# GpSimd forms the low parts of the blocks of w3 and the products r·k·u of three more chunks

## The chip, the cores and the metric

The kernel runs on one core of one Trainium2 chip. The metric is the device time of one execution in microseconds (us). The kernel before took 889.52 us (median of 3 runs, 889.01 to 890.25).

A core has five engines that each work through their own list of instructions in order and wait for one another by semaphores: TensorE (PE in the rows, its weight loads PEld), VectorE (DVE), ScalarE (ACT), GpSimd (POOL) and SyncE (SP), which here only issues DMAs.

## The reference

Three layers follow each other. A linear attention runs over 768 steps with a state per head:

```
for t in range(S):
    cur = einsum('bhd,bhe->bhde', u * k[t], v[t])
    y[t] = einsum('bhd,bhde->bhe', r[t], state + cur)
    state = w[t][..., None] * state + einsum('bhd,bhe->bhde', k[t], v[t])
```

Its output x (3072 rows of 384) goes through `h = ((x @ w1) * (x @ w2)) @ w3` and `h @ w_out`, and then through a mixture of eight experts with two chosen per row. All of it is float32.

## The kernel before

float32 matrices are multiplied in three passes. A matrix is split in a high part h (the value rounded to the narrower format `fp32r`) and a low part l = x - h, and `mm3` (lines 182 to 184) issues three matmuls: high by high, high by low, low by high. For each tile of a weight, ScalarE prepares the bits (`top`, line 153), VectorE joins them into a float (`cvz`, line 166), ScalarE rounds it (h, line 168), and VectorE subtracts (l, line 173). This is `cvt` with its queue `flush`: a call of `cvt` for the next tile first issues the join of the tile before and the subtraction of the tile before that.

The kernel folds w3 and w_out into one matrix first. In the loop over u (0 to 18) `cv_wo(u)` converts one of 8 blocks of w_out (`WBh`, `WBl`), `cv_w3(u)` one of 16 blocks of w3 (`w3h`, `w3l`, 128 x 512, three buffers each, with four buffers of `cvz`), and `mm_w3(u - 3)` multiplies: 12 matmuls of 400 columns, of which the four of line 184 read `w3l`. I count blocks of w3 from 0 to 15.

The attention works on 24 chunks of 128 steps, counted from 0 too, two per group of 256 rows. Steps of the first chunks are laid between the folding's by a table of times: `pre_scan` (`fg`), `pre_rec` (`rc`, `kt`), `pre_k`, `pre_r` (`rt`), then `pre_u` (lines 240 to 245), which forms r·k·u in two multiplications of 128 x 384 into the tile `rku` (one buffer), `pre_c` (line 250, `cc`, the sum over a head's columns), `pre_d` (line 256: ScalarE lays `cc` on the diagonals of `am`, eight instructions), `at_A` (line 263), `do_ov` (line 268, VectorE), `at_y` (line 332, the output, rounded into `xh` by ScalarE at line 338 and `xl` by VectorE at line 339) and `at_kv` (line 296, the state). After `pre_u(j)` follows the load of r and k for chunk j + 2 (`nrk`, two buffers). In the kernel before, VectorE forms the products for chunks 2, 3 and 4, GpSimd those of all others.

From 66 us on the groups' matmuls with w1, w2 and the folded matrix run (`mo_ab`, `mo_x`), in between the attention's; then the experts.

VectorE's instructions stand in the order in which the program issues them. Those of TensorE (until the third group), ScalarE, GpSimd and SyncE are put in order by a scheduler with costs of its own, so a changed engine for one instruction can reorder the others.

Of the kernel before, what the change touches and what calls it, by code (L numbers as in the profile page):

```python
# [16 lines left out]
OP = mybir.AluOpType  # L17
# [3 lines left out]
DM, FF, E = 384, 1024, 8  # L21
# [50 lines left out]
def tile_kernel(ctx: ExitStack, tc: tile.TileContext, dt, nat, w3t, wout, w1, w2, e1, e2, cf, ci, out):  # L72
    nc = tc.nc
    pe, act, dve, pool, sp = nc.tensor, nc.scalar, nc.vector, nc.gpsimd, nc.sync
# [6 lines left out]
    class Pinned:  # L81
        on = False
# [7 lines left out]
    def f(ap):  # L90
        return ap.bitcast(F32)
# [14 lines left out]
    def c(n):  # L106
        o, w = CF[n]
        return cft[:, o:o + w]
# [32 lines left out]

    CQ, LQ, TOP = [], [], [cvp.tile([P, 512], I32, name=f"top{i}", bufs=1) for i in range(2)]

    def cvt(rw, n, h, l, o=0, post=None):

        t = TOP[0][:, :n]
        TOP.append(TOP.pop(0))  # L150
        top = rw.bitcast(BF16)[:, 4 * o + 4:4 * o + 4 * n + 4].rearrange("p (n t) -> p n t", t=4)[:, :, 0]
        mid = rw[:, 2 * o + 1:2 * o + 2 * n + 1].rearrange("p (n t) -> p n t", t=2)[:, :, 0]
        act.activation(out=t.bitcast(F16).rearrange("p (n t) -> p n t", t=2)[:, :, 1], in_=top, func=AF.Copy)
        z = cvp.tile([P, 512], I32, name="cvz")[:, :n]
        if post == "z":
            dve.scalar_tensor_tensor(z, mid, 13, t, op0=OP.logical_shift_right, op1=OP.bitwise_or)
            return z.bitcast(F32)
        flush(1)
        CQ.append((mid, t, z, h, l, post))

    def flush(n=2):
        for _ in range(n):
            low, LQ[:] = LQ[:], []
            while CQ:
                mid, t, z, h, l, post = CQ.pop()
                dve.scalar_tensor_tensor(z, mid, 13, t, op0=OP.logical_shift_right, op1=OP.bitwise_or)  # L166
                x = z.bitcast(F32)
                (act.copy if xo_ else dve.tensor_copy)(out=h, in_=x)
                LQ.append((h, l, x))
                if post:  # L170
                    post(x)
            for h, l, x in low:
                dve.tensor_tensor(out=l, in0=x, in1=f(h), op=OP.subtract)  # L173

    def load64(rw, src):

# [10 lines left out]
    DT, RK, VV, FG, RC, KT, RT, AM, KN, XH, XL, KS = ({} for _ in range(12))  # L187
# [51 lines left out]

    def pre_u(j):  # L240
        t = att.tile([P, DM], F32, name="rku", bufs=1)
        on = dve if 2 <= j < 5 else pool
        on.tensor_tensor(out=t, in0=RK[j][:, :DM], in1=RK[j][:, DM:], op=OP.mult)  # L243
        on.tensor_tensor(out=t, in0=t, in1=c("u"), op=OP.mult)
        KS["u", j] = t

    def pre_c(j):
# [104 lines left out]
    def do_u(j):  # L352
        pre_u(j)
        if j + 2 < NCH:
            load_rk(j + 2)
# [29 lines left out]
    rawx, w3s, xo_, R1 = {}, {}, {}, {}  # L385
# [10 lines left out]
    def cv_wo(j):  # L396
        cvt(rawx["o", j], DM, woh[:, j, :DM], wol[:, j, :DM], post=lambda x: xo_.__setitem__(j, x))
# [18 lines left out]

    def cv_w3(u):
        w3s[u] = [fold.tile([P, 512], F32R, name=x, bufs=3) for x in ("w3h", "w3l")]
        cvt(rawx["3", u], 512, *w3s[u])

    def mm_w3(u):
        jb = u % 8
# [18 lines left out]
    def cv_w(m, fp, i):  # L441
        sl = slice(768 * fp + 384 * i, 768 * fp + 384 * i + 384)
        rw, o = piece(m, fp, i)
        cvt(rw, 384, (WAh, WBh)[m][:, sl], (WAl, WBl)[m][:, sl], o)

    def cv_early():
        flush(1)
        for i in range(2):
            rw, o = piece(1, 0, i)
            EZ.append(cvt(rw, 384, None, None, o, "z"))  # L450
# [51 lines left out]
    for i, fn in enumerate(STEPS):  # L502
        for j in range(NCH):
            late = 3 if j == NCH - 1 and i == 1 else 0
            at(WHEN[j][i] if j in WHEN else 6 * j - 14 + LATE[i] - late, fn, j)
    at(-3, flush)
    at(-3, flush, 1)
    for slot in (0.1, 2.55, 2.9, 3, 5, 5.3, 6.02, 6.04):
# [24 lines left out]
    for u in range(19):  # L533
        if u < 8:
            cv_wo(u)
            ld_raw()
        if u < 16:
            cv_w3(u)
            ld_raw()
        elif u == 16:  # L540
            flush()
        run_todo(u - 24, u - 23.5)
        if u > 2:
            mm_w3(u - 3)
        if 0 < u < 9:
            gate_cols(u - 1)
            gate_split(u - 1)
        if u == 1:
            warm_up(6)
        if u < 8:  # L550
            wo_T(u)
        if u == 0:
            warm_up(3)
        act.on = u >= 15
        run_todo(u - 23.5, u - 23)
# [591 lines left out]
    if RMAX > 1:  # L1147

        n = nc.values_load(rounds[0:1, E:E + 1], min_val=1, max_val=RMAX)
# [102 lines left out]
```

## Time and profile before

| | |
|---|---|
| median of 3 runs | 889.52 us |
| profiled execution | 888.03 us, its span 886.1 us |
| PE busy | 866.6 us (98%) |
| DVE busy | 496.2 us (56%) |
| ACT busy | 434.8 us (49%) |
| POOL busy | 244.2 us (28%) |

The span reaches from the first to the last instruction that the profiler saw. An engine's busy time counts its instructions alone, not its waits. Averages over the span say little about the first 112 us, to which the change belongs: there VectorE is busy most of the time and GpSimd hardly. The times of a row are from the span's start.

### The profile page before, as it was taken

How to read it: one execution, taken by the hardware profiler on the slowest of the kernel's cores; microseconds unless marked ns; L12 is line 12 of the kernel's file. 1: busy time of each engine (PE TensorE's matmuls, PEld its weight loads, DVE VectorE, ACT ScalarE, POOL GpSimd, SP SyncE). 2: the span in 40 equal slices, each digit the busy share in tenths (PEclk: the TensorE clock that was granted, in tenths of full speed). 3: DMA queues.
4: the chain of work that ended last, by engine and by line, in shares of the span. 5: the costliest groups of instructions: out<-in, count | busy, mean ns of one | idle time of the engine just before them, and what ended most of it. 6: DMA issues, size and time to landing. Idle time of an engine off the chain costs nothing.

```text
span 886.1 us, 18270 instructions
## 1 busy us (share of the span) xinstructions
PE 866.6 (98%) x7333; PEld 807.6 (91%) x7333; DVE 496.2 (56%) x1215; ACT 434.8 (49%) x876; POOL 244.2 (28%) x216
## 2 busy tenths in 40 slices
PE   8999999999999999999999999999999999999994
PEld 5889899999999999999989989899998989999894
DVE  6899866857756766666474453443434344353320
ACT  5787576566466546645454343334334343434320
POOL 2000020141131231231453434326061341604022
PEclk9999999999999999999999999999999999999998
DMA  9965398465475563525186786829287583835113
GB/s 344 405 221 178 99 135 267 119 201 162 129 205 170 157 170 109 147 70 157 43 205 126 177 244 190 196 83 226 57 228 138 145 202 91 221 76 110 18 22 38
DMA packets 123967, 139.22 MB, mean 157 GB/s; under 512 B 74976, under 2 KB 103648, under 8 KB 123872
## 3 DMA queue, kind: packets, MB, share of 16 engines
q1 hardware_dynamic: 100336, 109.58, 43.1%
q0 software_dynamic: 12160, 19.72, 11.9%
q10 hardware_dynamic: 11376, 8.65, 3.0%
q8 instruction: 59, 0.97, 0.5%
q14 instruction: 36, 0.29, 0.1%
HBM read 88.12 MB, written 36.04 MB: 140 GB/s over the span
## 4 chain that ended last, share of the span: by engine, by line
PE 87%; DVE 5%; DMA 3%; ACT 1%; issue 1%; POOL 0%; SPq 0%; POOLq 0%; ACTq 0%; DVEq 0%
PE pb L182 27%; PE pb L183 26%; PE pb L184 26%; PE pb L332 3%; PE pb L263 3%; DMA rawf<-wout 2%; PE pb L932 1%; DMA nrk<-nat 1%; PE pb L296 1%; DVE cvz L166 1%; DMA rawf<-w 1%; DVE am L268 0%; DVE WAl L173 0%; DVE fg L210 0%; DVE w3l L173 0%
## 5 line engine op out<-in xcount | busy, mean ns | idle before, releaser
L937 POOL DMA_INDIRECT out<-ye,ti x49 | 77.0, 1572 | 225.2 <-ACT ye L927 204.8
L910 DVE SCALAR_TENSOR_TENSOR HH<-pb,HH 128x256 fp32r<-128x256 f32 (+1 forms) x128 | 71.2, 557 | 112.3 <-ACT HH L909 112.3
L182 PE MATMUL pb<-XTh,WAh 128*128 128x512 f32 (+1 forms) x384 | 131.7, 343 | 0.0
L184 PE MATMUL pb<-XTh,WAl 128*128 128x512 f32 (+1 forms) x384 | 131.3, 342 | 0.0
L183 PE MATMUL pb<-XTl,WAh 128*128 128x512 f32 (+1 forms) x384 | 131.0, 341 | 0.0
L182 PE MATMUL pb<-WBh,HH 128*128 128x384 f32 x384 | 129.3, 337 | 0.0
L184 PE MATMUL pb<-WBh,HH 128*128 128x384 f32 x384 | 128.4, 334 | 0.0
L183 PE MATMUL pb<-WBl,HH 128*128 128x384 f32 x384 | 128.3, 334 | 0.0
L909 ACT ACTIVATE HH<-pb 128x256 fp32r<-128x256 f32 (+1 forms) x128 | 62.8, 492 | 115.4 <-PE pb L184 113.3
L742 POOL DMA_INDIRECT slots<-g_sc,g_si x48 | 51.6, 1074 | 127.1 <-DVE g_si L741 71.6
L927 ACT ACTIVATE ye<-pb,ti 128x384 f32<-128x384 f32 x42 | 24.4, 582 | 124.2 <-PE pb L184 124.2
L183 PE MATMUL pb<-xl,WAh 128*128 128x256 f32 x288 | 80.9, 281 | 0.8 <-DVE xl L339 0.8
L182 PE MATMUL pb<-xh,WAh 128*128 128x256 f32 x288 | 81.5, 284 | 0.0
L183 PE MATMUL pb<-xl,WBh 128*128 128x256 f32 x288 | 81.0, 281 | 0.0
L182 PE MATMUL pb<-xh,WBh 128*128 128x256 f32 x288 | 81.0, 281 | 0.0
L184 PE MATMUL pb<-xh,WBl 128*128 128x256 f32 x288 | 81.0, 281 | 0.0
L184 PE MATMUL pb<-xh,WAl 128*128 128x256 f32 x288 | 80.8, 281 | 0.0
L183 PEld LDWEIGHTS pb<-XTl,WAh 128*128 128x128 f32 x384 | 72.3, 188 | 7.6
L184 PEld LDWEIGHTS pb<-XTh,WAl 128*128 128x128 f32 x384 | 72.2, 188 | 7.5
L182 PEld LDWEIGHTS pb<-XTh,WAh 128*128 128x128 f32 x384 | 72.0, 188 | 7.5
L182 PEld LDWEIGHTS pb<-WBh,HH 128*128 128x128 f32 x384 | 72.1, 188 | 5.0 <-ACT WAh L810 4.4
L243 POOL TENSOR_TENSOR rku<-nrk 128x384 f32<-128x384 f32 x21 | 21.7, 1031 | 194.3 <-DVE cc L250 79.4
(203 smaller groups left out, 2065.1 us busy)
## 6 DMA issues: line engine op xcount, KB each, us to landing
dtc<-dt SPq DMA_DIRECT2D x24, 772.0 KB, 5.2
raw<-e SPq DMA_DIRECT2D x18, 768.0 KB, 5.9
raww<-e SPq DMA_DIRECT2D x14, 768.0 KB, 5.5
nrk<-nat SPq DMA_DIRECT2D x24, 384.0 KB, 5.5
expert_rows<-xg SPq DMA_DIRECT2D x45, 192.0 KB, 4.1
rawf<-w3t SPq DMA_DIRECT2D x16, 512.0 KB, 7.5
nv<-nat SPq DMA_DIRECT2D x24, 256.0 KB, 4.5
out<-zeros SPq DMA_DIRECT2D x9, 576.0 KB, 4.5
```

What stands on the lines that cost most here:

```text
L166: dve.scalar_tensor_tensor(z, mid, 13, t, op0=OP.logical_shift_right, op1=OP.bitwise_or)
L182: pin(pe.matmul(o, wh, xh, start=start, stop=False))
L183: pe.matmul(o, wh, xl, start=False, stop=False)
L184: pe.matmul(o, wl, xh, start=False, stop=stop)
L243: on.tensor_tensor(out=t, in0=RK[j][:, :DM], in1=RK[j][:, DM:], op=OP.mult)
L263: pe.matmul(bST[hb][:, P * a:P * a + P], KT[j][q, a].rearrange("p s i -> p (s i)"), RT[j][q, a].rearrange("p s i -> p (s i)"), start=True, ...
L332: pe.matmul(o, lt, rh, start=st, stop=en, tile_position=tp)
L742: ins = pool.indirect_dma_start(out=table, out_offset=bass.IndirectOffsetOnAxis(ap=si[:, i, k:k + 1], axis=0), in_=SC[:, i, k, :], in_offs ...
L909: act.activation(out=Hh[hf][:, ff], in_=bank[:, :n], func=AF.Relu)
L910: dve.scalar_tensor_tensor(Hl[hf][:, ff], bank[:, :n], 0.0, f(Hh[hf][:, ff]), op0=OP.max, op1=OP.subtract)
L927: act.activation(out=y[:n], in_=bank[:n], func=AF.Copy, scale=wt)
L937: ins = pool.indirect_dma_start(out=out, out_offset=bass.IndirectOffsetOnAxis(ap=ti(e, j)[:, 0:1], axis=0), in_=y[:n], in_offset=None, com ...
```

## The change

The subtraction of `w3l` goes from VectorE to GpSimd, for all 16 blocks; and the two multiplications of `pre_u` go from VectorE to GpSimd for chunks 2, 3 and 4.

```diff
-    def cvt(rw, n, h, l, o=0, post=None):
+    def cvt(rw, n, h, l, o=0, post=None, low=None):
...
-        CQ.append((mid, t, z, h, l, post))
+        CQ.append((mid, t, z, h, l, post, low or dve))
...
-            for h, l, x in low:
-                dve.tensor_tensor(out=l, in0=x, in1=f(h), op=OP.subtract)
+            for h, l, x, on in low:
+                on.tensor_tensor(out=l, in0=x, in1=f(h), op=OP.subtract)
...
-        on = dve if 2 <= j < 5 else pool
-        on.tensor_tensor(out=t, in0=RK[j][:, :DM], in1=RK[j][:, DM:], op=OP.mult)
-        on.tensor_tensor(out=t, in0=t, in1=c("u"), op=OP.mult)
+        pool.tensor_tensor(out=t, in0=RK[j][:, :DM], in1=RK[j][:, DM:], op=OP.mult)
+        pool.tensor_tensor(out=t, in0=t, in1=c("u"), op=OP.mult)
...
-        cvt(rawx["3", u], 512, *w3s[u])
+        cvt(rawx["3", u], 512, *w3s[u], low=pool)
```

GpSimd's list at its start, as a difference. A pair of L243 and L244 is the products of one chunk: the first pair those of chunk 0, the next those of chunk 1, and so on; L173 are the low parts in the order of the blocks.

```order
 L489 CAST trib<-cft 128x128
-L243 ISA
+L243 TENSOR_TENSOR rku<-nrk 128x384
+L173 TENSOR_TENSOR w3l<-cvz,w3h 128x512
+L244 TENSOR_TENSOR rku<-rku,cft 128x384
+L173 TENSOR_TENSOR w3l<-cvz,w3h 128x512 x7
+L243 TENSOR_TENSOR rku<-nrk 128x384
+L244 TENSOR_TENSOR rku<-rku,cft 128x384
+L243 TENSOR_TENSOR rku<-nrk 128x384
+L244 TENSOR_TENSOR rku<-rku,cft 128x384
+L173 TENSOR_TENSOR w3l<-cvz,w3h 128x512 x4
 L243 TENSOR_TENSOR rku<-nrk 128x384
```

Four low parts (blocks 0 to 3) stand ahead of this piece. So block 11's stands ahead of the products of chunk 1, and the products of chunk 2 stand ahead of the low parts of blocks 12 to 15. The tile `rku` has one buffer: the products of chunk 2 wait until VectorE has summed those of chunk 1.

VectorE's list before, where `cc` of chunk 1 is formed (cvz are here blocks 11, 12 and 13, w3l 10, 11 and 12):

```order
L166 SCALAR_TENSOR_TENSOR cvz<-rawf,top_112 128x512
L173 TENSOR_TENSOR w3l<-cvz,w3h 128x512
L237 SCALAR_TENSOR_TENSOR rt<-dtc,rc 128x4x64
L238 TENSOR_TENSOR rt<-dtc,fg 128x4x64
L250 TENSOR_REDUCE cc<-rku 128x8
L339 TENSOR_TENSOR xl<-pb_76,xh 128x3x128
L166 SCALAR_TENSOR_TENSOR cvz<-rawf,top_111 128x512
L173 TENSOR_TENSOR w3l<-cvz,w3h 128x512
L166 SCALAR_TENSOR_TENSOR cvz<-rawf,top_112 128x512
L173 TENSOR_TENSOR w3l<-cvz,w3h 128x512
L210 SCALAR_TENSOR_TENSOR fg<-dtc,d_64 128x520
```

The same place now:

```order
L166 SCALAR_TENSOR_TENSOR cvz<-rawf,top_112 128x512
L237 SCALAR_TENSOR_TENSOR rt<-dtc,rc 128x4x64
L238 TENSOR_TENSOR rt<-dtc,fg 128x4x64
L250 TENSOR_REDUCE cc<-rku 128x8
L339 TENSOR_TENSOR xl<-pb_76,xh 128x3x128
L166 SCALAR_TENSOR_TENSOR cvz<-rawf,top_111 128x512
L166 SCALAR_TENSOR_TENSOR cvz<-rawf,top_112 128x512
L210 SCALAR_TENSOR_TENSOR fg<-dtc,d_64 128x520
```

Only the subtractions are gone; `cc` of chunk 1 still stands ahead of the joins of blocks 12 and 13.

TensorE's list before, where it forms the output of chunk 0 (L332) beside block 10 (`w3h_516`, `w3l_517`):

```order
L182 MATMUL pb2_74<-WBh_69,w3h_516 128x400
L332 MATMUL pb4_76<-am_564,nv_204 32x128
L183 MATMUL pb2_74<-WBl_70,w3h_516 128x400
L182 MATMUL pb3_75<-WBh_69,w3h_516 128x400
L183 MATMUL pb3_75<-WBl_70,w3h_516 128x400
L332 MATMUL pb4_76<-am_564,nv_204 32x128 x15
L184 MATMUL pb0_72<-WBh_69,w3l_517 128x400
```

And now:

```order
L184 MATMUL pb0_72<-WBh_69,w3l_517 128x400
L182 MATMUL pb1_73<-WBh_69,w3h_516 128x400
L183 MATMUL pb1_73<-WBl_70,w3h_516 128x400
L184 MATMUL pb1_73<-WBh_69,w3l_517 128x400
L182 MATMUL pb2_74<-WBh_69,w3h_516 128x400
L183 MATMUL pb2_74<-WBl_70,w3h_516 128x400
L184 MATMUL pb2_74<-WBh_69,w3l_517 128x400
L182 MATMUL pb3_75<-WBh_69,w3h_516 128x400
L332 MATMUL pb4_76<-am_564,nv_204 32x128
L183 MATMUL pb3_75<-WBl_70,w3h_516 128x400
L184 MATMUL pb3_75<-WBh_69,w3l_517 128x400
L332 MATMUL pb4_76<-am_564,nv_204 32x128 x15
```

All four matmuls of line 184 of block 10 have come ahead of the output's last fifteen instructions.

## Rows read from the trace of the kernel before

**Rows 1.** Busy time in six stretches (engine busy us, instructions; clock; DMA)

```profile
8.00:44.00 36.00, 32.62 (x214) 27.47 (x213) 31.40 (x62) 26.71 (x58) 3.20 (x4) 1.00 1.03 407
44.00:63.00 19.00, 18.84 (x174) 15.97 (x176) 17.42 (x32) 15.03 (x34) 2.37 (x2) 1.00 0.62 228
80.00:112.00 32.00, 30.46 (x373) 27.80 (x373) 27.79 (x54) 20.16 (x49) 1.67 (x2) 1.00 0.37 114
112.00:850.00 738.00, 738.00 (x6249) 695.96 (x6249) 399.53 (x1028) 352.40 (x698) 223.32 (x190) 1.00 0.59 149
```

**Rows 2.** PE's waits, 8 to 62 us (line <- releaser: us, times, longest)

```profile
PE pb L182 <- ACT w3h L168: 1.4, 3, 1.0
PE pb L412 <- ACT top L153: 0.9, 1, 0.9
PE pb L183 <- DVE WBl L140: 0.9, 2, 0.6
```

**Rows 3.** Timeline of POOL (start us, us, instruction, idle before and releaser)

```profile
20.29 1.23 POOL L243 TENSOR_TENSOR rku<-nrk 128x384 f32<-128x384 f32 x1 [0.53 <-DMA nrk<-nat]
21.59 1.34 POOL L244 TENSOR_TENSOR rku<-rku,cft 128x384 f32<-128x384 f32 x1
43.84 1.18 POOL L243 TENSOR_TENSOR rku<-nrk 128x384 f32<-128x384 f32 x1 [20.90 <-DMA nrk<-nat]
45.10 1.34 POOL L244 TENSOR_TENSOR rku<-rku,cft 128x384 f32<-128x384 f32 x1
110.25 1.01 POOL L243 TENSOR_TENSOR rku<-nrk 128x384 f32<-128x384 f32 x1 [63.80 <-DVE cc L250]
```

**Rows 4.** Timeline of DVE beside POOL's products

```profile
20.70 1.37 DVE L173 TENSOR_TENSOR w3l<-cvz,w3h 128x512 fp32r<-128x512 f32 x1
22.54 0.95 DVE L166 SCALAR_TENSOR_TENSOR cvz<-rawf,top 128x512 int32<-128x512 int32 x1
44.06 1.51 DVE L173 TENSOR_TENSOR w3l<-cvz,w3h 128x512 fp32r<-128x512 f32 x1
45.76 1.35 DVE L268 COPY_PREDICATED am<-cit,pb 128x512 f32<-128x512 int32 x2
```

**Rows 5.** Timeline of DVE, 49 to 68 us

```profile
49.12 0.68 DVE L166 SCALAR_TENSOR_TENSOR cvz<-rawf,top 128x512 int32<-128x512 int32 x1
51.00 0.54 DVE L250 TENSOR_REDUCE cc<-rku 128x8 f32<-128x384 f32 x1
53.93 0.69 DVE L173 TENSOR_TENSOR w3l<-cvz,w3h 128x512 fp32r<-128x512 f32 x1
59.17 1.35 DVE L268 COPY_PREDICATED am<-cit,pb 128x512 f32<-128x512 int32 x2
62.08 0.68 DVE L173 TENSOR_TENSOR w3l<-cvz,w3h 128x512 fp32r<-128x512 f32 x1
62.68 0.55 DVE L166 SCALAR_TENSOR_TENSOR cvz<-raw,top 128x384 int32<-128x384 int32 x1
67.49 0.55 DVE L339 TENSOR_TENSOR xl<-pb,xh 128x384 fp32r<-128x384 f32 x1
```

**Rows 6.** Timeline of ACT, 50 to 52 us

```profile
50.58 0.48 ACT L338 CAST xh<-pb 128x384 fp32r<-128x384 f32 x1 [3.12 <-PE pb L332]
50.95 0.62 ACT L168 CAST w3h<-cvz 128x512 fp32r<-128x512 f32 x1
```

**Rows 7.** Timeline of PE: output of chunk 0, block 11, first group

```profile
51.92 0.34 PE L183 MATMUL pb<-WBl,w3h 128*128 128x400 f32 x1
52.10 0.34 PE L182 MATMUL pb<-WBh,w3h 128*128 128x400 f32 x1
68.09 0.39 PE L183 MATMUL pb<-xl,WAh 128*128 128x256 f32 x1 [0.79 <-DVE xl L339]
```

**Rows 8.** PE's waits, 80 to 112 us

```profile
PE pb L296 <- ACT kn L275: 0.7, 1, 0.7
PE pb L263 <- DVE rt L238: 0.4, 1, 0.4
PE pb L273 <- DVE xl L339: 0.3, 1, 0.3
```

**Rows 9.** Groups of DVE's instructions, 80 to 112 us (count | busy us, mean ns)

```profile
L244 DVE TENSOR_TENSOR rku<-rku,cft 128x384 f32<-128x384 f32 x3 | 1.7, 558 | 0.1
L243 DVE TENSOR_TENSOR rku<-nrk 128x384 f32<-128x384 f32 x3 | 1.6, 547 | 0.0
```

**Rows 10.** Timeline of SP's issues: r and k of chunk 3, then w1

```profile
45.05 0.33 SPq L195 DMA_DIRECT2D nrk<-nat  x1
45.43 0.42 SPq L178 DMA_DIRECT2D raw<-w  x1
```

**Rows 11.** DMA issues by line (count, KB each, median us to landing)

```profile
raw<-w SPq DMA_DIRECT2D x6, 768.0 KB, 5.4
```

More of the change, by code (lines that the diff above doesn't have):

```diff
@@ L164, in flush @@
             while CQ:
-                mid, t, z, h, l, post = CQ.pop()
+                mid, t, z, h, l, post, on = CQ.pop()
                 dve.scalar_tensor_tensor(z, mid, 13, t, op0=OP.logical_shift_right, op1=OP.bitwise_or)
@@ L168, in flush @@
                 (act.copy if xo_ else dve.tensor_copy)(out=h, in_=x)
-                LQ.append((h, l, x))
+                LQ.append((h, l, x, on))
                 if post:
                     post(x)
-            for h, l, x in low:
-                dve.tensor_tensor(out=l, in0=x, in1=f(h), op=OP.subtract)
+            for h, l, x, on in low:
+                on.tensor_tensor(out=l, in0=x, in1=f(h), op=OP.subtract)
     def load64(rw, src):
```

## Prediction

> **What bounds the kernel now.** I read the busy time by stretches first [rows 1]. From 112 to 850 us TensorE (PE) is busy 738.00 us of 738.00: a microsecond that PE loses or wins before 112 us stays lost or won. So the question is only what happens to PE before 112 us. From 8 to 44 us PE is busy 32.62 of 36 us beside a VectorE (DVE) at 31.40; from 44 to 63 us it is busy 18.84 of 19, beside a DVE at 17.42; from 80 to 112 us 30.46 of 32. DVE is well filled in all three, but PE waits little: taking work off DVE can win at most those 3.4, 0.2 and 1.5 us. Second, PE's own waits [rows 2, 8]: before 62 us 0.9 us for a low part of WB, 1.4 and 0.9 us for ScalarE (ACT). No wait for w3l stands among them.
>
> Third, the places where GpSimd (POOL) already works beside DVE [rows 3, 4]. DVE's w3l at 20.70 took 1.37 us, at 44.06 1.51 us; the undisturbed ones at 53.93 and 62.08 took 0.69 and 0.68 [rows 5]. In the first case POOL's product ended at 20.29 + 1.23 = 21.52 and w3l at 22.07; in the second at 45.02 and 45.57: both 0.55 us after POOL's end. The join at 22.54 ended at 23.49, 0.56 us after POOL's 22.93. The reverse holds too: the products at 21.59, 43.84 and 45.10 were not done in the 1.01 us of the one at 110.25, but 0.86 to 0.87 us after DVE's instruction had ended (22.07 to 22.93; 45.57 to 46.44). So in these rows a DVE instruction that reads two tensors in SBUF and a POOL product run one after the other, never together. The predicated copies at 45.76, which read PSUM, took 1.35 us beside POOL, the same as at 59.17 alone: those are not held up. I read a product of 384 columns as 0.14 us of start and a hold of 0.87 us.
>
> **The change part by part.**
>
> *Prices.* A low part of 128 x 512 on POOL is shown by no row. Bounds: 1.01 us (as the product of 384 columns alone) and 1.34 x 512/384 = 1.79 us (the longest product, scaled). I take 0.14 + 0.87 x 512/384 = 1.30 us, a hold of 1.16, since all four disturbed products agree with the 0.87. On DVE a w3l costs 62.68 - 62.08 = 0.60 us of its list [rows 5].
>
> *Front, blocks 0 to 10 (8 to 50 us).* DVE loses 11 x 0.60 = 6.6 us of work, and POOL holds 11 x 1.16 = 12.8 us. Over the four products of rows 3 (holds 3.48 us) DVE lost 0.68 + 0.26 + 0.82 + 0 = 1.76 us, one half. Half of 12.8 is 6.4 us: nothing is won or lost. Bounds: a gain of 3.2 us (all the waits of rows 2) and a loss of 12.8 - 6.6 = 6.2 us. I take 0. That w3l comes 0.6 us later than before costs nothing while PE has the block's eight matmuls with w3h to do first.
>
> *Term A, the sum cc of chunk 1.* Before, its products ran on POOL from 43.84 to 46.44, when r and k had landed, and DVE read them at 51.00 without waiting [rows 3, 5]. Now POOL's list has the low part of block 11 ahead of them. That needs the rounded w3h of block 11, which ACT formed at 50.95 to 51.57, behind xh of chunk 0, for which it had waited 3.12 us for PE [rows 6]. PE's output of chunk 0 now stands behind all four matmuls with block 10's low part: 4 x 0.18 us (the distance of two matmuls, 51.92 to 52.10 [rows 7]) = 0.73 us later. So w3h of block 11 is there at 52.3, its low part at 52.3 + 1.30 = 53.6, the two products (DVE stands still, so 1.01 us each and about 0.07 between) at 55.7. cc starts at 55.7 instead of 51.0: DVE stands, +4.7 us. Behind it on DVE are xl of chunk 0, the joins of blocks 12 to 15 and then the conversion of w1; ACT waits for cc (the diagonals) and for the joins. Bounds: 2.6 us (a low part of 1.01 us, PE's 0.73 not added, and ACT rounding w3h as soon as its join ends, 49.12 + 0.68 = 49.8 [rows 5], 1.1 us sooner: 4.7 - 0.3 - 0.7 - 1.1) and 5.9 us (1.79 for the low part, 1.34 for each product).
>
> *Term B, from cc to xl of chunk 1 (67.49 before).* POOL now does the products of chunk 2, which wait for cc, and after them the low parts of blocks 12 to 15: at the soonest 55.7 + 0.55 + 2.1 + 1.3 = 59.6 for block 12's, against 53.93 + 0.69 = 54.6 before. PE runs out of other work there, since it was busy 18.84 of 19 us with just these blocks. DVE loses five w3l, 3.0 us, and meets six holds, 2 x 0.87 + 4 x 1.16 = 6.4 us. The first four (4.1 us) fall on a join, a join, the scan and a small product, all with two operands in SBUF: less the start-ups some 3.4 us are lost. Of the last two, half, 1.2. Term B is 3.4 + 1.2 - 3.0 = +1.6 us; bounds 0.2 (half of all holds) and 3.4 (all of them). The trace shows blocking until the end and no partial speed. The Trainium skill, "SBUF — State Buffer", section "Who interferes with whom", says the same in its strict form: a DVE instruction with two SBUF inputs contends with a GpSimd instruction that reads SBUF, and whoever comes second waits for the whole instruction. By that rule alone, with each hold met, the sum below would end at 6.9 instead of 5.1 us; by the share of the trace's four products at 3.7.
>
> PE takes the delay over one for one: at 68.09 it waited 0.79 us for that xl [rows 7].
>
> *Term C, 80 to 112 us.* DVE loses three pairs of products, 1.6 + 1.7 = 3.3 us [rows 9]. PE waits there 0.7 + 0.3 us at the end of the chain cc, diagonals, output, xl, state, and 0.4 us for rt [rows 8], which stand right behind the second and third pair. These 1.4 us can go; against them the products of chunk 3 now hold DVE up when it is full. I take -1.2 us; bounds -1.5 and 0.
>
> *At nothing.* SyncE's load of r and k for chunk 3 waits for the products of chunk 1 to have read their buffer; it was issued at 45.05 and now at about 54.7, and the loads of w1 and w2 queued behind it move as much [rows 10]. They are hidden: such a load takes 5.4 us [rows 11], so it lands at about 61; the join at 62.68 [rows 5] is of the w1 loaded before it, and those of this load follow that one, themselves some 5 us late. Without that cover it would cost what the landing exceeds 68 us.
>
> Sum: 0 + 4.7 + 1.6 - 1.2 = +5.1 us. The profiled execution took 888.03 us, so 893.1 for it; the median of the runs shown is 1.49 us higher, and I predict for that: 889.5 + 5.1 = **894.6 us**.
>
> **Rivals.**
>
> *DVE's relief reaches PE (faster).* Place: all of 8 to 112 us. DVE's list is shorter by 16 x 0.60 + 3.3 = 12.9 us, and the waits that DVE and the engines behind it give PE are 3.2 us before 62 us and 1.4 after 80. If half of their 4.6 us goes, 887.2 us. For it: DVE is 87% to 92% busy there, and the copies from PSUM show that it can work beside POOL. Against it: PE's own bound of 18.84 in 19 us, and POOL's list. It decides itself at cc of chunk 1: only if the products are done by 51 us is there a gain.
>
> *The stall is hidden (same).* If ACT rounds w3h of block 11 before it waits for PE and the low part is short, term A is at its lower bound; with B and C at theirs the sum is 2.6 + 0.2 - 1.5 = 1.3: 890.8 us. Against it: ACT's list has xh first.
>
> *Every hold is paid (slower still).* If low parts of 512 columns take 1.79 us, blocks 12 to 15 follow each other at POOL's pace: A at 5.9, B at 3.4 and the front at half of its bound give 5.9 + 3.4 + 3.1 - 1.2 = 11.2: 900.7 us. For it: w3h waits for its third buffer, which POOL now frees, and joins wait for their fourth.
>
> **How the numbers follow.** My forecast has a chance of 0.66, with its own range 892.1 to 897.7: A and B half way to their bounds (3.65 to 5.3 and 0.9 to 2.5) give 892.9 to 896.1, the front a quarter of the way (-0.8 and +1.6) the rest. Paid holds 0.14, hidden 0.10, relief 0.10. To hold 8 in 10, the range goes from 891.0 to 899.0: it leaves out the relief and much of the paid holds. A change of 0.2% (1.8 us) is about what a measurement of this kernel can tell: faster 0.10, the same 0.11, slower 0.79.
>
> **What would show it.** In the profile after: POOL's products of chunk 1 start near 53.6 us, and DVE's largest wait is cc on POOL's rku, 4 to 5 us; w3l stands 16 times on POOL at a mean of about 1.3 to 1.4 us; PE's busy time in 44 to 63 us falls by some 4 us, with waits for POOL's w3l of block 12; xl of chunk 1 starts near 73 to 74 us; the issue at 45.05 moves to about 55; and every row after 112 us stands about 5 us later. I am wrong if cc starts before 52 us, or if PE shows no idle time between 50 and 62 us.

## The result and the profile after

The changed kernel takes **896.03 us** (median of 6 runs, 894.41 to 897.67) beside 889.06 us for the kernel before (6 runs, 887.89 to 890.25): slower, ratio 1.0082, 95% interval 1.0065 to 1.0098. That is +6.97 us; predicted were +5.1, and 896.03 lies in the range. The profiled execution took 896.3 us with a span of 894.5, 8.4 longer than the span of before.

The busy time by stretches, as [rows 1], and two stretches of 2 us for the clock (after the engines: the granted clock, the share of the DMA engines, GB/s):

```profile
8.00:44.00 36.00, 31.05 (x183) 26.64 (x182) 28.97 (x48) 23.88 (x53) 15.29 (x12) 0.95 1.01 394
44.00:63.00 19.00, 14.71 (x139) 11.65 (x136) 13.40 (x21) 11.52 (x28) 9.53 (x8) 1.00 0.35 133
80.00:112.00 32.00, 30.99 (x371) 28.31 (x370) 27.65 (x53) 23.70 (x54) 4.63 (x4) 1.00 0.40 137
112.00:850.00 738.00, 737.50 (x6256) 694.83 (x6255) 400.41 (x1025) 353.29 (x701) 223.06 (x191) 1.00 0.58 150
34.00:36.00 2.00, 2.00 (x8) 1.88 (x8) 2.00 (x3) 1.63 (x3) 1.33 (x1) 0.50 1.03 427
```

As before, nothing is lost or won from 112 us on. From 44 to 63 us PE is busy 14.71 us, 4.13 less than before. In the front it is busy 31.05 instead of 32.62, and for some of that at the lower of its two clock levels: 8 matmuls in 2 us at 34 us. All rows of before stand at 1.00 there.

PE's waits from 8 to 62 us, as [rows 2], which sum to 3.2 us; these four sum to 8.2:

```profile
PE pb L182 <- ACT w3h L168: 3.6, 4, 1.2
PE pb L183 <- DVE WBl L140: 1.9, 2, 1.2
PE pb L402 <- DVE cvz L166: 1.4, 2, 0.8
PE pb L184 <- POOL w3l L173: 1.3, 3, 0.5
```

POOL's timeline, as [rows 3], from block 11's low part to block 12's, and the group of its low parts (count | busy us, mean ns of one | idle before them):

```profile
55.23 1.29 POOL L173 TENSOR_TENSOR w3l<-cvz,w3h 128x512 fp32r<-128x512 f32 x1 [4.83 <-ACT w3h L168]
56.46 1.02 POOL L243 TENSOR_TENSOR rku<-nrk 128x384 f32<-128x384 f32 x1
57.56 1.01 POOL L244 TENSOR_TENSOR rku<-rku,cft 128x384 f32<-128x384 f32 x1
...
61.60 1.72 POOL L173 TENSOR_TENSOR w3l<-cvz,w3h 128x512 fp32r<-128x512 f32 x1
```

```profile
L173 POOL TENSOR_TENSOR w3l<-cvz,w3h 128x512 fp32r<-128x512 f32 x16 | 22.2, 1389 | 37.4 <-ACT w3h L168 28.7 <-ACT WBh L139 7.2 <-ACT w3h L86 1.6
```

What releases block 11's low part, ACT's timeline as [rows 6]:

```profile
54.15 0.48 ACT L338 CAST xh<-pb 128x384 fp32r<-128x384 f32 x1 [3.69 <-PE pb L332]
54.53 0.62 ACT L168 CAST w3h<-cvz 128x512 fp32r<-128x512 f32 x1
```

And DVE's timeline, as [rows 4, 5]: two held instructions of the front, a wait that is new there, `cc` of chunk 1, the held scan behind it, `xl` of chunk 1:

```profile
10.56 0.56 DVE L405 COPY woT<-pb 128x384 f32<-128x384 f32 x1 [0.56 <-PE pb L402]
...
16.77 2.35 DVE L210 TENSOR_TENSOR_SCAN fg<-dtc,d 128x520 f32<-128x520 f32 x1
...
39.95 1.71 DVE L166 SCALAR_TENSOR_TENSOR cvz<-rawf,top 128x512 int32<-128x512 int32 x1
...
58.61 0.55 DVE L250 TENSOR_REDUCE cc<-rku 128x8 f32<-128x384 f32 x1 [4.86 <-POOL rku L244]
...
62.11 2.30 DVE L210 TENSOR_TENSOR_SCAN fg<-dtc,d 128x520 f32<-128x520 f32 x1
...
75.81 0.55 DVE L339 TENSOR_TENSOR xl<-pb,xh 128x384 fp32r<-128x384 f32 x1
```

The first scan in the kernel before:

```profile
17.25 1.23 DVE L210 TENSOR_TENSOR_SCAN fg<-dtc,d 128x520 f32<-128x520 f32 x1
```

The chain of term A is there row by row: `xh` of chunk 0 late behind PE, then w3h of block 11, then its low part, then the two products, then `cc`, 4.86 us waited. `cc` starts at 58.61 instead of 51.00 and `xl` at 75.81 instead of 67.49, 8.32 us late, and that stays to the end.

The same places show where the 8.32 us were lost. `xh` of chunk 0 is 3.57 us late (54.15 against 50.58), the wait for the products brings `cc` to +7.61 (4.04 more), and the stretch to `xl` adds 0.71. Of the 3.57, 0.73 belong to term A by its own working: the four matmuls with block 10's low part that now stand ahead of the output. So in the terms of the forecast the profile shows 2.84 for the front, 4.77 for A and 0.71 for B.

### The profile page after: what moved, and what is told of

Its sections match the earlier page's. It is cut to its first block, busy times and chain, and to the rows that moved or that the text cites. A ratio compares the mean times of both kernels' runs of the same rounds, so it can differ in the third digit from the quotient of the medians.

```text
span 894.5 us, 18284 instructions
## 1 busy us (share of the span) xinstructions
PE 868.8 (97%) x7333; PEld 809.3 (90%) x7333; DVE 494.4 (55%) x1193; ACT 435.0 (49%) x876; POOL 270.8 (30%) x238
## 4 chain that ended last, share of the span: by engine, by line
PE 87%; DVE 5%; ACT 2%; issue 2%; POOL 1%; DMA 1%; SPq 0%; POOLq 0%; ACTq 0%; DVEq 0%
PE pb L182 26%; PE pb L184 26%; PE pb L183 26%; PE pb L332 4%; PE pb L263 3%; PE pb L932 1%; DVE cvz L166 1%; DVE fg L210 1%; POOL w3l L173 1%; PE pb L296 1%; DMA rawf<-wout 1%; ACT top L153 0%; DVE rc L227 0%; ACT w3h L168 0%; DVE WAl L173 0%
## 5 line engine op out<-in xcount | busy, mean ns | idle before, releaser
L813 DVE TENSOR_TENSOR WAl<-raww,WAh 128x768 fp32r<-128x768 f32 x28 | 26.8, 959 | 85.7 <-ACT WAh L810 85.7
```

Of the source, the lines that this page charges most:

```text
L813: dve.tensor_tensor(out=l, in0=src, in1=f(h), op=OP.subtract)
```

## Experiments

Twelve kernels; each stands beside runs of the kernel before on the same chip. "cc" and "xl" are the places of these two instructions of chunk 1 against the profile of before (51.00 and 67.49 us).

| run | median us (n) | before, us | ratio [95%] | cc, us | xl, us |
|---|---|---|---|---|---|
| whole change | 896.03 (6) | 889.06 | 1.0082 [1.0065, 1.0098] | +7.61 | +8.32 |
| e1 low parts only | 896.94 (6) | 889.70 | 1.0095 [1.006, 1.013] | +6.95 | +7.29 |
| e2 products only | 890.06 (12) | 889.70 | 1.0007 [0.9994, 1.0019] | +0.62 | +0.65 |
| e3 list pinned | 899.09 (6) | 889.70 | 1.0105 [1.0084, 1.0126] | +3.21 | +9.91 |
| e4 blocks 0 to 7 | 891.68 (12) | 889.70 | 1.0022 [1.001, 1.0033] | +4.16 | +3.97 |
| e5 blocks 8 to 15 | 894.14 (6) | 889.09 | 1.006 [1.0047, 1.0072] | +5.14 | +5.48 |
| e6 chunk 1 on DVE | 893.57 (6) | 889.09 | 1.0061 [1.004, 1.0083] | +2.48 | +3.97 |
| e7 e4 with fillers | 891.18 (12) | 889.09 | 1.0026 [1.0012, 1.004] | +1.91 | +1.94 |
| e8 extra subtractions | 897.35 (6) | 889.09 | 1.0115 [1.0086, 1.0144] | +5.69 | +5.79 |
| e9 chunks 0 to 4 on DVE | 893.81 (6) | 888.09 | 1.0063 [1.005, 1.0076] | +2.90 | +3.63 |
| e10 change with fillers | 895.79 (6) | 888.09 | 1.0082 [1.0068, 1.0095] | +5.32 | +6.04 |
| e11 e6, later | 895.17 (6) | 889.87 | 1.0059 [1.0039, 1.008] | +3.22 | +6.01 |
| e12 e9, later | 891.07 (12) | 889.87 | 1.0019 [1.0006, 1.0031] | +0.23 | +1.18 |

The places are those of one profiled execution each, the medians those of all. The profiles of e4 (893.79), e5 and e7 are of their slowest runs, those of e8, e9 and e10 of their fastest.

### The parts: e1, e2, e4, e5

e1, the low parts alone: `on = dve if 2 <= j < 5 else pool` again in `pre_u`.

> Only the 16 low parts of w3 go to GpSimd; the products of chunks 2 to 4 stay on VectorE. Two theories. Queue: what costs is GpSimd's list, in which the low part of block 11 stands ahead of the products of chunk 1, so that cc of chunk 1 stalls VectorE. That stall is still here (4 to 5 us in VectorE's wait for GpSimd's L244), but the products of chunk 2 no longer stand ahead of block 12; with the loss before 44 us I expect 893.5 to 895.5 us. Port: what costs is that GpSimd and VectorE hold each other up; then only the holds of six products go, and the time is within 1 us of the full change, 895 to 897 us.

It carries the whole loss. The wait is the same without the products of chunk 2 to 4:

```profile
57.95 0.55 DVE L250 TENSOR_REDUCE cc<-rku 128x8 f32<-128x384 f32 x1 [4.86 <-POOL rku L244]
```

e2, the products alone: `cvt(rawx["3", u], 512, *w3s[u])` again in `cv_w3`.

> Only the products of chunks 2 to 4 go to GpSimd; the low parts of w3 stay on VectorE. Queue: nothing stands ahead of the products, so no stall, and the waits of TensorE at 98 to 110 us shrink: 888.0 to 889.0 us. Port: six holds of 0.87 us against six instructions of 0.5 us on VectorE, which is full where two of the three pairs fall: 889.0 to 890.5 us.

No difference that can be measured; what was hoped of 80 to 112 us did not come. PE's waits there, as [rows 8]:

```profile
PE pb L263 <- DVE am L268: 0.8, 1, 0.8
PE pb L263 <- DVE rt L238: 0.4, 1, 0.4
```

The waits for `kn` (0.7) and `xl` (0.3) of [rows 8] are gone, and one for `am` (0.8) has come: PE is busy 30.50 us of 32 instead of 30.46.

e4, the front alone:

```diff
-        cvt(rawx["3", u], 512, *w3s[u], low=pool)
+        cvt(rawx["3", u], 512, *w3s[u], low=pool if u < 8 else None)
```

with the products as before.

> Only the low parts of blocks 0 to 7 go to GpSimd; blocks 8 to 15 and the products of chunks 2 to 4 stay on VectorE. This is the front alone. My prediction put it at nothing: 889 to 890 us. The profile of the full change puts it at up to 3.7 us by 44 us (W0l at 44.43 instead of 40.75), with TensorE's granted clock at half from about 34 to 37 us: 891.5 to 893 us. If the clock drop is what makes the front's loss, the granted clock of 32 to 40 us is below 1.00 here too; if the holds alone make it, the time rises without it.

2.0 us slower, so the front does cost. In its profile all of it is there before `cc` of chunk 1, and stays (+3.97 at `xl` and still at `cc` of chunk 2). Here too the clock falls:

```profile
34.00:36.00 2.00, 2.00 (x8) 1.99 (x8) 2.00 (x6) 1.50 (x4) 0.73 (x1) 0.50 1.05 429
36.00:38.00 2.00, 2.00 (x9) 1.79 (x9) 1.52 (x3) 0.24 (x1) 0.75 (x1) 0.50 0.98 383
```

e5, the other half: `low=None if u < 8 else pool`.

> The low parts of blocks 8 to 15 alone on GpSimd; blocks 0 to 7 and all products as before. The terms of the front and of chunk 1 add up: with all sixteen +7.3 us and with blocks 0 to 7 alone +2 to +4, so +4 to +5 here, 893.5 to 895, with cc of chunk 1 waiting 4 to 5 us for GpSimd and no stretch at 0.50 before 40 us. Rival, the two overlap (the wait for the products exists whatever the front did and is the whole cost): 896 to 897.

As the adding theory said: 894.14, and `cc` waits 4.10 us for POOL although blocks 0 to 7 are converted as before:

```profile
56.14 0.55 DVE L250 TENSOR_REDUCE cc<-rku 128x8 f32<-128x384 f32 x1 [4.10 <-POOL rku L244]
```

That there would be no stretch at 0.50 before 40 us was wrong: the clock stood at 0.50 from 32 to 34 us here too, well before the first low part on POOL (40.70). This profile shows what the lower clock alone can do. Up to 31 us PE stands as in the kernel before (0.25 us at 28.91 and 0.91 us at 31.15 beside 0.26 and 0.92 there), and `cc` of chunk 0 starts at 34.53 beside 34.48. Then a low part of WB, which comes by way of PE, is 1.63 us late. The row of e5, then that of before:

```profile
38.11 0.17 DVE L140 TENSOR_TENSOR WBl<-pb,WBh 128x16 fp32r<-128x16 f32 x1 [1.97 <-ACT WBh L139]
```

```profile
36.48 0.17 DVE L140 TENSOR_TENSOR WBl<-pb,WBh 128x16 fp32r<-128x16 f32 x1 [0.39 <-ACT WBh L139]
```

The two halves add up: 1.98 + 5.05 = 7.03 beside 7.24 for all sixteen, though the interval of the sixteen is wide (5.3 to 11.6 us).

### The wait of cc: e3, e6, e11

e3 keeps the whole change and pins POOL's list, the products of chunk 1 between blocks 8 and 9:

```diff
-                on.tensor_tensor(out=l, in0=x, in1=f(h), op=OP.subtract)
+                low = on.tensor_tensor(out=l, in0=x, in1=f(h), op=OP.subtract)
+                if on is pool:
+                    tc.keep_in_program_order(low)
...
-        pool.tensor_tensor(out=t, in0=RK[j][:, :DM], in1=RK[j][:, DM:], op=OP.mult)
-        pool.tensor_tensor(out=t, in0=t, in1=c("u"), op=OP.mult)
+        pin = tc.keep_in_program_order if j < 3 else lambda x: x
+        pin(pool.tensor_tensor(out=t, in0=RK[j][:, :DM], in1=RK[j][:, DM:], op=OP.mult))
+        pin(pool.tensor_tensor(out=t, in0=t, in1=c("u"), op=OP.mult))
```

and `pre_u(1)` in the table of times from -14.5 to -13.5.

> The whole change, but with GpSimd's list kept in an order in which the products of chunk 1 stand between the low parts of blocks 8 and 9, and those of chunk 2 behind block 15. The same instructions on the same engines. Queue: VectorE's wait of 4.9 us for GpSimd at cc goes, and block 12's low part comes at once: 4 to 5 us below the full change, 891 to 892 us. Port: the holds are all still there, the delay only moves: 895 to 896 us.

A miss: the wait of `cc` is gone, the kernel is slower than the change. The scheduler had also put `at_A` of chunk 1 ahead of four low matmuls, as in the kernel before but not in the change, and PE (line 266 is 263 here) stood for `rt`, then worked at the lower clock:

```profile
54.34 2.08 PE L266 MATMUL pb<-rt,kt 48*128 48x128 f32 x16 [3.19 <-DVE rt L240]
```

So it does not tell what the wait costs. e6 takes the wait away differently. From e1:

```diff
-        on = dve if 2 <= j < 5 else pool
+        on = dve if 1 <= j < 5 else pool
```

> All sixteen low parts on GpSimd as in the run with the low parts only (896.94), but the products of chunk 1 on VectorE as well, so that VectorE's reduction to cc of chunk 1 has no semaphore of GpSimd's queue to wait for. The queue theory (cc stood 4.9 us only because block 11's low part stands ahead of chunk 1's products on GpSimd): cc goes early again, the 4.9 us go, two products of some 0.7 us come to VectorE, so 3 to 4 us back: 893 to 894. Rival, low parts and holds on the path whatever cc waits for: within 1 us of the run with the low parts only, 896 to 897.5.

893.57: against e1 some 2.8 us back (4.48 over before instead of 7.24). But the two products, now in DVE's list, brought a stall of their own, and PE waited behind it; DVE's row, then PE's:

```profile
43.79 0.56 DVE L243 TENSOR_TENSOR rku<-nrk 128x384 f32<-128x384 f32 x1 [1.51 <-DMA nrk<-nat]
```

```profile
46.09 0.70 PE L182 MATMUL pb<-WBh,w3h 128*128 128x400 f32 x1 [2.86 <-DVE W0l L140]
```

e11 is e6 with `pre_u(1)` at -12.4 in the table, so that the products stand behind `W0l` and the masks of chunk 0.

> As the run with all low parts on GpSimd and the products of chunk 1 on VectorE (893.57), whose trace showed VectorE 1.5 us before the load of r and k of chunk 1 and TensorE 2.9 us for the low part of W0 behind it, with the clock at 0.50 after that; here these two products stand behind the low part of W0 and the masks of chunk 0. If that stall of VectorE's queue was the rest of the loss, it goes: 891 to 892.3, the loss of the front alone. Rival, the low parts of blocks 8 to 15 cost of themselves (held VectorE, late delivery): 893 to 894.5.

The stall went, the time did not: 895.17. `cc` starts at 54.22, 3.73 us sooner than in e1, but `xl` only 1.28 sooner. What is late next is PE, which waits for the blocks themselves and then runs at 0.50 from about 57 to 60 us, and DVE waits for the state that PE forms behind them; PE's rows, then DVE's:

```profile
54.70 0.45 PE L182 MATMUL pb<-WBh,w3h 128*128 128x400 f32 x1 [1.11 <-ACT w3h L168]
...
56.06 0.45 PE L184 MATMUL pb<-WBh,w3l 128*128 128x400 f32 x1 [0.73 <-POOL w3l L173]
...
63.52 0.55 PE L296 MATMUL pb<-nv,kn 128*32 128x48 f32 x32
```

```profile
64.13 0.36 DVE L303 TENSOR_TENSOR stmp<-pb,snew 128x192 f32<-128x192 f32 x1 [4.13 <-PE pb L296]
```

By the medians, taking the wait of 4.9 us away is therefore worth 2 to 3 us (1.9 by e11, 2.8 by e6); under it lies a PE that is late for the blocks of w3 anyhow. Neither difference is clear of the noise, for e1's interval reaches from 5.3 to 11.6 us. Both edits also moved other instructions, so the share is no finer than that.

### Holds, clock and the way back: e7 to e10, e12

e8 is the kernel before with eight more subtractions on POOL, of the operands of blocks 0 to 7, into a scratch that nobody reads; DVE forms all low parts as before. With `low=pool if u < 8` again, in the loop of `flush`:

```diff
-                on.tensor_tensor(out=l, in0=x, in1=f(h), op=OP.subtract)
+                for on, l in ((dve, l), (pool, WAl[:, :512]))[:1 + (on is pool)]: on.tensor_tensor(out=l, in0=x, in1=f(h), op=OP.subtract)
```

> The kernel before, with eight extra GpSimd subtractions of the sizes and operands of the low parts of blocks 0 to 7, written to a scratch that nobody reads; VectorE forms all low parts itself as before. Hold theory (what costs is that VectorE's two-operand instructions stand while GpSimd's runs): VectorE loses some 1 us at each of the places where the front is bound by it, 891 to 893. Rival, what costs is that GpSimd's low parts come late to TensorE, or its late release of buffers: 889.5 to 890.3 if only the delivery matters.

More than the hold theory gave: 897.35, +8.26. In the front of this profile no compute engine waits for POOL; DVE's instructions are longer. DVE, then POOL's instruction beside the first of them:

```profile
17.21 2.32 DVE L210 TENSOR_TENSOR_SCAN fg<-dtc,d 128x520 f32<-128x520 f32 x1
...
37.72 1.78 DVE L173 TENSOR_TENSOR w3l<-cvz,w3h 128x512 fp32r<-128x512 f32 x1
```

```profile
16.64 1.79 POOL L173 TENSOR_TENSOR WAl<-cvz,w3h 128x512 fp32r<-128x512 f32 x1 [1.78 <-ACT w3h L168]
```

The scan took 1.23 us alone (at the same place before) and ended 1.10 after POOL here; POOL's own 1.79 us contain its wait for DVE's subtraction at 16.60. The eight holds, with a fall of the clock that was there too in this profile (0.50 from 32 to 34 us), cost this kernel far more than it takes (e4, +1.98) when DVE is also rid of the eight subtractions.

e7 asks whether the lower clock makes the front's loss: e4 with two throw-away matmuls at four places.

```diff
-        if u == 0:
-            warm_up(3)
+        if u in (W := {0: 3, 5: 2, 6: 2, 7: 2, 8: 2}):
+            warm_up(W[u])
```

> The kernel with the low parts of blocks 0 to 7 alone on GpSimd (891.68, granted clock 0.50 from about 32.6 to 39.9 us), with two throw-away bf16 matmuls on TensorE at four places of 26 to 42 us, of which the order of TensorE's other work is little changed before 38 us. Clock theory (the lower clock makes most of the loss of the front): no stretch at 0.50, and 889.5 to 890.5. Rival, the late low parts and held VectorE instructions make it and the clock only falls because of them: clock back or not, 891.3 to 892.3.

The clock stayed up, and the ratio is the same as e4's (1.0026 beside 1.0022):

```profile
34.00:36.00 2.00, 2.00 (x15) 1.55 (x13) 2.00 (x4) 1.59 (x4) 1.34 (x1) 1.00 1.03 428
```

In its profile `xl` is only 1.94 us late instead of 3.97, but both rest on one execution; this one then stood 3.30 us at 489 us for a gathered tile, far from the change. e10 puts the same matmuls into the whole change.

> The whole change with eight throw-away bf16 matmuls on TensorE at four places of 26 to 42 us, as in the run that put them into the kernel with blocks 0 to 7 (there no stretch at the lower clock before 60 us, mean granted clock 0.995 instead of 0.993, 0.5 us back). If the lower clock at 34 to 37 us is a part of the loss of the whole change, 894.3 to 895.7 beside its 896.0, and no stretch at 0.50 before 44 us. Rival (the waits for GpSimd end last whatever the clock does): 895.8 to 897.

Again the clock is at 1.00 from 34 to 36 us and the ratio is unchanged, 1.0082 both. `cc` still waits for POOL:

```profile
56.32 0.55 DVE L250 TENSOR_REDUCE cc<-rku 128x8 f32<-128x384 f32 x1 [4.14 <-POOL rku L244]
```

That profile is of e10's fastest run, with a mean granted clock of 0.996. Four of the other five stand at 0.991 or 0.992, so in them the fillers hardly kept the clock up throughout. In e7 ten of twelve runs stand at 0.995 or 0.996, where e4 has ten of twelve at 0.991 to 0.994. There the median gains nothing, but the fillers take time of PE themselves (0.59 us a pair), and the two intervals (0.9 to 2.9 us for e4, 1.1 to 3.6 for e7) leave room for a microsecond. So the medians show no separate price of the lower clock and do not exclude one. The profiles point to one: 1.63 us in e5, and `xl` 2.0 and 2.3 us sooner in e7 and e10 than in e4 and the change.

e9 goes the other way: the kernel before with the products of chunks 0 and 1 on DVE too, `on = dve if j < 5 else pool`.

> The kernel before with the opposite change: the products of r, k and u of chunks 0 and 1 go from GpSimd to VectorE too, so that GpSimd holds VectorE nowhere before 112 us. Hold theory (an instruction moved to GpSimd takes from VectorE about as long as it gives it): no loss, 888.3 to 889.7 beside about 889.3 for the kernel before. Rival (VectorE is bound before 68 us and pays each added product in full): four products of some 0.45 us, 1 to 2 us slower, 890.3 to 891.5.

A miss, 5.7 us slower, and mostly not for DVE's work. The products of chunk 1 stand at a place of DVE's list that it reaches 4 us before their data; `W0l` stands behind them. DVE's row, then PE's:

```profile
43.01 0.56 DVE L243 TENSOR_TENSOR rku<-nrk 128x384 f32<-128x384 f32 x1 [3.98 <-DMA nrk<-nat]
```

```profile
45.90 0.70 PE L182 MATMUL pb<-WBh,w3h 128*128 128x400 f32 x1 [4.53 <-DVE W0l L140]
```

On POOL the same wait of 20.90 us in [rows 3] had cost nothing, because nothing was queued behind it. e12 moves these two to -12.4.

> As the run with the products of chunks 0 to 4 all on VectorE (893.81), whose trace showed VectorE 4.0 us before the load of r and k of chunk 1 with the low part of W0 behind it; here the products of chunk 1 stand behind that low part. Without the stall the hold theory gives no loss against the kernel before, 888 to 889.5 (two holds of some 0.85 us gone at 43 to 46 us, two products of some 0.5 us come). Rival, VectorE's own work is the price: 889.8 to 891.

The stall is gone, and with it 4.5 of the 5.7 us: 891.07, ratio 1.0019. `am` of chunk 0 starts 0.83 us sooner than before, so the front does gain without POOL; then the products' 1.1 us put w3l of two blocks behind PE, which waits for it:

```profile
50.70 0.99 PE L184 MATMUL pb<-WBh,w3l 128*128 128x400 f32 x4 [1.13 <-DVE w3l L173]
53.49 0.64 PE L184 MATMUL pb<-WBh,w3l 128*128 128x400 f32 x2 [1.07 <-DVE w3l L173]
```

That is the upper end of the rival's range, which made DVE's own work the price; the hold theory's 888 to 889.5 did not come. No division between POOL and DVE that was tried beats the kernel before.

## Why the prediction was right, and where it was not

**What bounds the kernel** held: 737.50 of 738 us from 112 us on, and what PE had lost at `xl` of chunk 1 (8.32 us) is lost at the end (8.4).

**Prices** held: 1.28 to 1.30 us for an undisturbed low part (1.30 predicted), a mean of 1389 ns with the holds. The rule of the Trainium skill, "SBUF — State Buffer", section "Who interferes with whom", that whoever comes second waits for the whole instruction, agrees with the scan at 16.77 (1.23 us alone, 2.35 beside POOL's 1.29) and with POOL's 1.79 us in e8.

**Term A**: the mechanism is right in each step, DVE waits 4.86 us, and the term itself is 4.77 (4.7 predicted): `cc` falls 4.04 us further behind than `xh` of chunk 0, and 0.73 lie ahead of `xh`. As a term of a sum it was probably too large: taken away it gives back 2 to 3 us in the medians (e6, e11, not clear of the noise), and the rows of e11 show a PE that is late for the blocks beside it. **Term B** was 0.71 us in the profile of after and 0.34 in e1 and e5 (where DVE keeps the products of chunk 2), 1.6 predicted. Together A and B were forecast at 6.3; the late half alone cost 5.05 in the medians (e5), with an interval of 4.2 to 6.4.

**The front** is the step that failed: "nothing is won or lost" was wrong by 2.0 us in e4's median, 2.84 us in the profile of after at `xh` of chunk 0. Part of the 2.84 is probably the lower clock from 34 us on, which the forecast did not have; with the clock up, in e7's profile, 1.94 us are left. The half of the holds was right: eight long rows of DVE between 16 and 51 us are 7.6 us longer than their like alone, 6.8 of it by low parts, where 6.4 were predicted. What failed was to set the 6.6 us of saved work against it at full value. DVE, relieved, came to the copies `woT` before PE had transposed for them: the row at 10.56 is one of four, 2.3 us in all, none of them in the trace of before, and DVE's busy time fell by 2.43 us from 8 to 44 us while its wait grew. A saving ahead of a wait is lost in it; the holds on the scan, `rc`, `rt` and the joins stand on the way to `WBl`, w3h and `W0l`, for which PE waits. DVE's `rc` and PE's wait behind it, in the profile of after (0.69 us for that `rc` before, no hold):

```profile
30.88 1.66 DVE L227 SCALAR_TENSOR_TENSOR rc<-kt,rc 128x512 f32<-128x512 f32 x1
...
32.46 0.16 DVE L140 TENSOR_TENSOR WBl<-pb,WBh 128x16 fp32r<-128x16 f32 x1
```

```profile
32.68 0.45 PE L183 MATMUL pb<-WBl,w3h 128*128 128x400 f32 x1 [1.20 <-DVE WBl L140]
```

e8, with the holds and without the saving, shows the one side of this, e4 the other.

**Term C** was forecast at -1.2 and did not come (e2, 1.0007): PE's waits changed their owner, from `kn` and `xl` to `am`. The upper bound, 0, was the right value.

**At nothing**: the load of r and k of chunk 3 was issued at 57.51, and PE has no new wait for w1 behind it, so it was hidden as said.

**Rivals.** Relief reached PE nowhere, and the stall was not hidden. "Every hold is paid" (900.7) did not come: the low parts behind `cc` took at most 1.72 us, and before 62 us the profile shows no compute engine waiting for a buffer that POOL frees: only DVE's `cc` and PE's matmuls with `w3l` wait for POOL. The forecast was 1.4 us low: the front is missing (+2.0), C (-1.2) did not come, and A with B cost less than 6.3. Errors of both signs lie behind the range that held, so that it held is in part luck.

**Open.** What the lower clock costs is not separated from the holds (e5's profile against e7's and e10's medians). How far the late blocks and how far the clock delay PE between 54 and 61 us in e11 was not separated, and why e8's median lies 3.6 us above its own profile neither: its runs with a mean granted clock of 0.985 to 0.988 took 899 to 903 us, those of 0.991 to 0.993 took 894 to 896.

## What to carry to other kernels

Work that is moved to an engine that holds the first one up, as POOL and DVE do here, must be counted twice: the holds fall on whatever stands in the other engine's list at that time, often on the chain, while the work saved is only worth what is left after the next wait on that list. Before an instruction moves into another in-order list, ask when its data are there and what stands behind it: 20.90 us of waiting were free on GpSimd, 3.98 us on VectorE cost 4.5 (e9 less e12). And a wait of 4.9 us need not come back whole when it is removed (2 to 3 us here); look what is late under it.

## What was not expected of the hardware

TensorE's granted clock fell from 1.00 to 0.50 (2.4 to 1.2 GHz) in the folding, behind stretches in which PE stood: in the profile of after at 34 us, behind waits of 0.65, 0.61 and 1.20 us between 26 and 33 us; in e9 behind one of 4.53 us, in e6 of 2.86 us. The waits do not decide it alone: in e5 it fell at 32 us behind 0.25 and 0.91 us, and in the kernel before it stayed at 1.00 behind 0.26 and 0.92 us at the same places. The distance of two matmuls was then 0.33 instead of 0.18 us, for some 3 to 7 us. With eight throw-away matmuls of 512 columns it stayed at 1.00 there in the two profiled executions (e7, e10); the medians gained nothing.

At about 490 us PE waited for a gathered tile, 3.30 us in e7's profile, 1.1 in e4's, not at all in that of before: two executions differ there by more than some of the effects above.
